# Sparse attention and a squared-ReLU MLP on one core: batch 3's strided heads on quarters of the array, wider sums and wider scaling

## The chip, the cores and the metric

The kernel runs on one core of one Trainium2 chip. The core has a matrix engine (TensorE, PE in the profile, with its weight loads as PEld), a vector engine (VectorE, DVE), a scalar engine for table functions (ScalarE, ACT), GpSimd (POOL), which here mostly issues transfers with a change of type, and SyncE (SP), which issues the other transfers and the transposes done by DMA. PSUM holds TensorE's results in eight banks of 512 fp32 columns by 128 partitions. The metric is the device time of one execution in microseconds; lower is better.

## The reference

Attention over 8 batches of 8 heads, 576 positions, head size 64, then an MLP over the 4608 resulting rows:

```python
rel = pos[:, None] - pos[None, :]
mask_local = (rel >= 0) & (rel < 32)
mask_strided = (rel >= 0) & (pos[None, :] % 32 == pos[:, None] % 32)
# heads 0..3 use mask_local, heads 4..7 mask_strided
attn = softmax(where(mask, 0.125 * q @ k.T, -1e9))
x = (attn @ v).transpose(0, 2, 1, 3).reshape(4608, 512)
r = maximum(x @ w_in, 0)          # w_in 512 x 2048
out = (r * r) @ w_out             # w_out 2048 x 512
```

A local head attends to the last 32 positions only. A strided head splits into 32 residue classes of 18 positions each; a position attends to the earlier ones of its own class. The kernel skips the rest.

## The kernel before

**Order of the work.** The MLP runs in nine chunks of 512 rows. A chunk has 16 groups of the first product (line 864: four matmuls of 512 columns into one bank, then a Relu on ScalarE, line 870, and a square on VectorE, line 874) and 16 of the second (line 970: four matmuls each; four groups make one output tile, copied by ScalarE, line 974, and stored over SP). These groups are numbered from 0 on, 32 to a chunk: groups 96 to 111 are the first product of chunk 3. The attention of batches 1 to 7 is cut into steps, and the text `PLAN`, written out by hand, says ahead of which group each step is issued. Batch b must be through before the chunk that holds its rows: batch 2 before group 64 (chunk 2), batch 3 before 96 (chunk 3), batch 4 before 128 (chunk 4). The chunk reads the strided rows of x, `xt[2]` and `xt[3]`, with the third and fourth matmul of a group. `tick()` runs after each group; `later(n, ...)` and `put_off(n, ...)` hold back a piece of a step by n groups, which the plan gives as numbers behind a plus sign.

**Banks.** Banks 4 and 5 alternate for the groups of both products. The other six are handed out in turn, singly (`bank`) or as neighbours (`bank_two`), to the attention steps.

**Strided heads, two ways.** The old way (batches 1 and 3, `OLD`) keeps K and V of two residue classes as block-diagonal 128 x 128 weights. `step_SS` (s3.0, s3.1, s3.2 in the plan) makes the scores of 8, 8 and 6 blocks of 54 columns with full-array matmuls (line 624) and takes Exp; `step_XX` (x3.0, x3.1, x3.2) makes the sums by one matmul with a block of ones (line 635), the values by one matmul a block (line 638), then 1/sum as Exp(-Ln(sum)) (lines 641, 643) and the products with it into `xt` (lines 651, 658). Two copies by VectorE fill the block-diagonal K (`step_K`, lines 380, 384) and two the V (`spread_v_str`, line 445).

The new way (batches 2, 4, 5, 6, 7) uses 64 x 64 quarters of the array, four matmuls at a time for four residue classes. `step_S4` makes 32 + 12 score matmuls (lines 688, 693) and three Exp; `step_X4` has three parts of 16, 16 and 12 value matmuls (line 757), each with four matmuls of ones for the sums (line 752) that share the bank of the values. `finish` then does, per part, Ln and Exp (lines 723, 724) and the products (line 736 for parts 0 and 1, six of 64 x 144 each; line 729 for part 2, four of 64 x 162). V comes by four DMAs into one of the two tiles of `vs_pool` (lines 430, 434); the old way takes two DMAs into a tile of its own (lines 438, 441).

**Local heads.** `step_G` makes the scores of four local heads with 24 matmuls into six banks (line 597), with six Exp (line 607) and the masks (line 604). `step_D` multiplies by V (line 823) and divides (lines 828, 829); `step_E` transposes into `xt` by DMA on SP from batch 2 on (line 838). `shift_v_local` (line 458) copies the 32 rows of V that overlap. In the plan, units 4b and 4b+1 are the two pairs of local heads of batch b: D16.0 is batch 4's first pair, first head.

The lines of the plan around the change (before):

```python
72: Q21k s3.0
...
75: x3.0
...
88: x3.1
90: x3.2
...
94: G4
...
99: X5k D16.0 D16.1
```

Of the kernel before, what the change touches and what calls it, by code (L numbers as in the profile page):

```python
# [8 lines left out]
FP32 = mybir.dt.float32  # L9
BF16 = mybir.dt.bfloat16  # L10
AF = mybir.ActivationFunctionType
# [51 lines left out]
50: Q17q Q16q s2  # L63
52: Q17k
55: X3k X3q
56: C4k C4q x2+2+4
57: V3 R12kv
58: V4 R12qa
60: B30v
61: B31v R13qv  # L70
62: R13ka
63: U4
64: X4q
66: Y17
67: Y16 C5q
68: k30v
69: k31v
70: X4k
71: C5k Q20k Q21q Q20q
72: Q21k s3.0  # L80
73: s3.1
75: x3.0
76: s3.2
80: G3
81: H3v
84: D12.0 D13.0
85: D12.1 D13.1
86: E12
87: E13
88: x3.1  # L90
90: x3.2
93: H4v
94: G4
96: k41v
97: Y20 Y21
98: U5
99: X5k D16.0 D16.1
100: C6k
101: X5q
102: Q25q V5  # L100
103: C6q
104: E16
106: s4 Q25k
107: D17.0
109: Q24k Q24q D17.1
111: E17
113: x4+2+5
114: k51v
122: G5
124: V6  # L110
127: H5v
# [5 lines left out]
138: D21.0  # L117
139: Q29k Q29q D21.1
142: E21
144: x5+2+5  # L120
150: H6v
152: k61v
154: G6
# [6 lines left out]
173: Y28  # L130
174: E24 D25.0 D25.1
175: Y29
176: x6+3+6
178: E25
187: H7v
188: G7
# [4 lines left out]
200: D28.1 E28  # L141
204: D29.1
206: E29
208: x7+4+8
"""

@with_exitstack
def kernel(
# [9 lines left out]
    nc = tc.nc  # L158
# [8 lines left out]
    NJ = 8  # L167
# [5 lines left out]
    NP2 = STRIDE // 2  # L173
    NG = 5
    NH = NG + 1
    OLD = (1, 3)
    NB = NP2 + NH
    NS = NP2 // 2
    W3 = 3 * NA
# [8 lines left out]
    att = ctx.enter_context(ExitStack())  # L188
    rows = ctx.enter_context(ExitStack())
    att_singles = att.enter_context(tc.tile_pool(name="att_singles", bufs=1))  # L190
    rv_pool = att.enter_context(tc.tile_pool(name="rv_pool", bufs=3))
    xl_pool = att.enter_context(tc.tile_pool(name="xl_pool", bufs=4))
    vs_pool = att.enter_context(tc.tile_pool(name="vs_pool", bufs=2))
    row_singles = rows.enter_context(tc.tile_pool(name="row_singles", bufs=1, side="right"))
# [27 lines left out]
    def bank_two():  # L222

        l = [id(t) for t in banks["pt"]]
        i = min((i for i in (0, 2, 6) if all(id(all_banks[i + j]) in l for j in range(2))),
                key=lambda i: max(l.index(id(all_banks[i + j])) for j in range(2)))
        for t in all_banks[i:i + 2]:
            k = [id(t) for t in banks["pt"]].index(id(t))
            banks["pt"].append(banks["pt"].pop(k))
            while id(t) in unread:  # L230
                run_due(lambda x: x[1] == unread[id(t)])
        return all_banks[i:i + 2], psb[:, i:i + 2]
# [27 lines left out]
    ones = singles.tile([128, D], BF16)  # L260
# [164 lines left out]
    def load_v_str(b):  # L425
        if b not in OLD:
            t = vs_pool.tile([128, (2 * NS + NH) * D], BF16, name="v_s")
# [186 lines left out]
    def blocks(part):  # L614
        return range(NJ * part, min(NJ * (part + 1), NB))
# [14 lines left out]
    def step_XX(b, part):  # L630
        run_due(lambda x: x[1] == (b, part))
        vb, n = vbd, len(blocks(part))
        e = es[2 + b % 2][:, NJ * W3 * part:NJ * W3 * part + W3 * n]
        pn, po = bank("pt")[:, 0:W3 * n], bank("pt")
        nc.tensor.matmul(pn, ones_bd, e, start=True, stop=True)
        for i, t in enumerate(blocks(part)):
            c = slice(W3 * i, W3 * (i + 1))
            nc.tensor.matmul(po[:, c], vb[:, t, :], e[:, c], start=True, stop=True)  # L638
        rv = rv_pool.tile([128, NJ * W3], FP32, name="rv")[:, 0:W3 * n]
        order = dict(a=n, h=3)  # L640
        nc.scalar.activation(rv.rearrange("c (h m a) -> c h m a", **order),
                             pn.rearrange("c (a h m) -> c h m a", **order), AF.Ln)
        nc.scalar.activation(rv, rv, AF.Exp, scale=-1.0)  # L643
        for h in (3,) if part == 2 else range(3):
            for par in range(2):
                r, x = slice(64 * par, 64 * par + 64), slice(64 * (h % 2), 64 * (h % 2) + 64)
                to = xt[2 + h // 2][x, b * S:(b + 1) * S].rearrange("c (m a r) -> c m a r", a=NP2, r=2)
                if part < 2:
                    of = po[r, 0:W3 * n].rearrange("c (a h m) -> c h m a", **order)[:, h]
                    by = rv[r].rearrange("c (h m a) -> c h m a", **order)[:, h]  # L650
                    nc.vector.tensor_tensor(to[:, :, NJ * part:NJ * (part + 1), par], of, by, op=ALU.mult)  # L651
                    continue
                of = po[r, 0:W3 * n].rearrange("c (a h m) -> c h m a", **order)
                by = rv[r].rearrange("c (h m a) -> c h m a", **order)
                for lo, g, k in ((0, 0, NG), (NG, 2, 1)):
                    t = to[:, :, 2 * NG * (g == 2) + lo, par]
                    t = bass.AP(t.tensor, t.offset, [t.ap[0], [2 * NG, 3 - g], [STRIDE, NA], [2, k]])
                    nc.vector.tensor_tensor(t, of[:, g:, :, lo:lo + k], by[:, g:, :, lo:lo + k], op=ALU.mult)
# [3 lines left out]
    def half(f, n=64):  # L662
        return slice(64 * f, 64 * f + n)
# [44 lines left out]
    def step_X4(b, pace):  # L708
        for part in range(3):
            run_due(lambda x: x[1] == ("s", b, part))  # L710
        for part in range(3):
            run_due(lambda x: x[1] == (b, part))
        e, vs = es[2 + b % 2], v_str[b]
        xb = slice(b * S, (b + 1) * S)

        def finish(part, n, both):
            w = n * W3
            rv = rv_pool.tile([128, NS * W3], FP32, name="rv")[:, 0:2 * w]
            pn = both[:, :, w:2 * w]
            o = "c (x f a) -> c f a x" if part < 2 else "c (f x a) -> c f a x"  # L720
            o, i = o.replace("f a x", "x f a") if part < 2 else o.replace("f a x", "f x a"), "c f (a x) -> c f a x"
            i = i.replace("c f a x", "c x f a" if part < 2 else "c f x a")
            nc.scalar.activation(rv.rearrange(o, f=2, a=n), pn.rearrange(i, a=n), AF.Ln)
            nc.scalar.activation(rv, rv, AF.Exp, scale=-1.0)  # L724
            if part == 2:
                for f, par in QUADS:
                    t = xt[3][64:128, xb]
                    t = bass.AP(t.tensor, t.offset + 2 * n * f + par, [t.ap[0], [2 * NG, 3], [STRIDE, NA], [2, n]])
                    nc.vector.tensor_tensor(t, both[half(par), f, 0:w].rearrange("c (a g m) -> c g m a", a=n, g=3),
                                            rv[half(par), w * f:w * (f + 1)].rearrange("c (g m a) -> c g m a", a=n, g=3),  # L730
                                            op=ALU.mult)
                return
            for h in range(3):
                for par in range(2):
                    to = xt[2 + h // 2][half(h % 2), xb].rearrange("c (m f a r) -> c m f a r", f=2, a=NS, r=2)
                    nc.vector.tensor_tensor(  # L736
                        to[:, :, :, n * part:n * (part + 1), par],
                        both[half(par), :, 0:w].rearrange("c f (a h m) -> c h m f a", a=n, h=3)[:, h],
                        rv[half(par)].rearrange("c (h m f a) -> c h m f a", h=3, f=2, a=n)[:, h], op=ALU.mult)

        due = []
        for part in range(3):
            n = (NS // 2, NS // 2, NH // 2)[part]
            w = n * W3
            pos, both = bank_two()

            def ecols(par, lo, k):
                c = NS * par + n * part + lo if part < 2 else 2 * NS + n * par + lo
                return slice(W3 * c, W3 * (c + k))

            for f, par in QUADS:
                nc.tensor.matmul(pos[f][half(par), w:2 * w], ones[half(f, W3)], e[half(f, W3), ecols(par, 0, n)],  # L752
                                 start=True, stop=True)
            for t in range(n):
                for f, par in QUADS:
                    r = 2 * (n * part + t if part < 2 else NS + t) + par
                    nc.tensor.matmul(pos[f][half(par), W3 * t:W3 * (t + 1)], vs[half(f, W3), D * r:D * (r + 1)],  # L757
                                     e[half(f, W3), ecols(par, t, 1)], start=True, stop=True)
            due.append((pace[part], pos, ("x", b, part), lambda part=part, n=n, both=both: finish(part, n, both)))
        for x in due:  # L760
            put_off(*x)

# [411 lines left out]
    for line in PLAN.strip().splitlines():  # L1174
        n, words = line.split(":")
# [42 lines left out]
```

## Time and profile before

| | us |
|---|---|
| median of 3 runs | 296.41 (296.08 to 297.07) |
| the profiled execution | 295.6 |
| its span, first to last instruction | 293.9 |
| TensorE busy (matmuls) | 286.8 |
| VectorE busy | 205.9 |
| ScalarE busy | 169.2 |
| GpSimd busy | 85.2 |

The profiled execution is one run; its span leaves out what lies before the first and after the last instruction. The granted clock of TensorE is full throughout (1.0). Matmuls overlap, so the mean duration of one is longer than the time from one to the next; the chain of work, which follows back from the last instruction what each piece waited for, gives the time that a piece adds. Names in the rows are those of the program: `psb` is PSUM, `xt` the MLP's input, `e` the exponentials, `rv` the reciprocals of the sums, `vb` and `kb` the block-diagonal weights.

### The profile page before, as it was taken

The page shows a single profiled execution, that of the slowest core. Times are in us where ns is not written, and L with a number is a line of the kernel's source. Part 1 is how long each engine was busy: PE and PEld are TensorE (multiplying, and loading weights), DVE is VectorE, ACT ScalarE, POOL GpSimd, SP SyncE. Part 2 cuts the span into 40 slices and gives each one's busy share as a digit, 9 for nine tenths or more (in the row PEclk, how much of TensorE's full clock was granted, in tenths as well). Part 3 has the DMA queues.
Part 4 walks back from the last instruction along what each step waited for, and adds up shares of the span by engine and source line. Part 5 has one row for each costly group of instructions (what it writes and reads, how often), then busy time and mean ns, then how long its engine had stood idle before and what let it go on. Part 6 is the DMA issues. An engine that isn't in the chain of part 4 may idle for free.

```text
span 293.9 us, 6454 instructions
## 1 busy us (share of the span) xinstructions
PE 286.8 (98%) x2477; PEld 153.0 (52%) x2477; DVE 205.9 (70%) x530; ACT 169.2 (58%) x318; POOL 85.2 (29%) x133
## 2 busy tenths in 40 slices
PE   6899999999999999999999999999999999999994
PEld 2554555544445454454445444444444444984594
DVE  5667798776587756667366826683389979958983
ACT  4767846684668736674577446654665566206610
POOL 8974442062116009246501740000000014103300
PEclk9999999999999999999999999999999999999999
DMA  7999999999999999999999999531011110030003
GB/s 151 180 209 207 197 203 180 159 243 127 153 220 130 172 163 185 164 129 125 217 204 109 158 183 165 86 58 74 36 20 55 75 38 0 1 117 30 0 2 143
DMA packets 91086, 37.23 MB, mean 127 GB/s; under 512 B 77392, under 2 KB 83896, under 8 KB 91056
## 3 DMA queue, kind: packets, MB, share of 16 engines
q0 software_dynamic: 49968, 18.14, 58.3%
q1 hardware_dynamic: 40944, 18.62, 34.0%
q8 instruction: 19, 0.31, 0.4%
q14 instruction: 11, 0.09, 0.1%
q10 hardware_dynamic: 144, 0.07, 0.1%
HBM read 36.83 MB, written 9.44 MB: 157 GB/s over the span
## 4 chain that ended last, share of the span: by engine, by line
PE 96%; DMA 2%; DVE 0%; issue 0%; DVEq 0%; POOLq 0%
PE psb L864 43%; PE psb L970 33%; PE psb L940 9%; DMA w_out_b<-in_q_dram 2%; PE psb L823 2%; PE psb L597 1%; PE psb L552 1%; PE psb L500 1%; PE psb L752 1%; PE psb L688 1%; PE psb L522 1%; PE psb L757 1%; PE psb L345 0%; PE psb L638 0%; PE psb L845 0%; PE psb L624 0%
## 5 line engine op out<-in xcount | busy, mean ns | idle before, releaser
L864 PE MATMUL psb<-xt,w_in 128*128 128x512 bf16 x576 | 131.9, 379 | 0.0
L870 ACT ACTIVATE r<-psb 128x512 bf16<-128x512 f32 x144 | 85.5, 598 | 46.0 <-PE psb L864 43.8
L970 PE MATMUL psb<-w_out_b,g_sb 128*128 128x512 bf16 x448 | 101.4, 379 | 0.0
L864 PEld LDWEIGHTS <-w_in 128*128 128x128 bf16 x576 | 53.8, 98 | 60.0 <-issue 0.8
L874 DVE TENSOR_TENSOR g_sb<-r 128x512 bf16<-128x512 bf16 x112 | 46.5, 422 | 39.9 <-ACT r L870 38.9
L970 PEld LDWEIGHTS <-g_sb 128*128 128x128 bf16 x448 | 41.8, 98 | 47.2
L974 ACT COPY y<-psb 128x512 f32<-128x512 f32 x28 | 16.6, 592 | 38.8 <-PE psb L970 38.7
L909 POOL CAST sa<-g_sb 128x256 fp32r<-128x256 bf16 x16 | 9.7, 605 | 96.5 <-DVE g_sb L904 96.5
L736 DVE TENSOR_TENSOR xt<-psb,rv 64x144 bf16<-64x144 f32 x60 | 18.7, 312 | 7.1 <-ACT rv L724 6.3
L604 DVE TENSOR_TENSOR e<-e,mask_all 128x576 bf16<-128x576 bf16 x24 | 10.0, 455 | 10.8 <-ACT e L607 10.7
L607 ACT ACTIVATE e<-psb 128x384 bf16<-128x384 f32 x36 | 15.0, 506 | 4.2 <-PE psb L597 4.2
L829 DVE TENSOR_TENSOR x_l<-psb,rinv 96x384 bf16<-96x384 f32 x28 | 15.5, 554 | 1.0
L904 DVE TENSOR_TENSOR g_sb<-r 128x512 bf16<-128x512 bf16 x32 | 13.0, 419 | 2.9 <-ACT r L870 2.9
L292 POOL DMA_DIRECT2D q_l<-in_q_dram x16 | 11.9, 749 | 9.3 <-PE psb L693 4.0
L363 POOL DMA_DIRECT2D q_t<-in_q_dram x6 | 3.2, 537 | 37.2 <-DMA qT_s<-q_t 35.5
L292 POOL DMA_DIRECT2D k_l<-in_k_dram x16 | 11.8, 741 | 1.5 <-issue 0.9
L940 PE MATMUL psb<-t,s 128*128 128x256 f32 x96 | 12.2, 283 | 0.0
L363 POOL DMA_DIRECT2D k_t<-in_k_dram x6 | 3.2, 538 | 30.1 <-DMA kT_s<-k_t 28.4
L940 PEld LDWEIGHTS psb<-t,s 128*128 128x128 f32 x96 | 11.6, 189 | 0.0
L952 DVE TENSOR_TENSOR y<-psb,y 128x256 f32<-128x256 f32 x19 | 8.1, 424 | 4.3 <-PE psb L940 3.5
L651 DVE TENSOR_TENSOR xt<-psb,rv 64x144 bf16<-64x144 f32 x24 | 7.5, 312 | 4.5 <-ACT rv L643 4.2
L823 PEld LDWEIGHTS <-e 128*128 128x128 bf16 x168 | 8.1, 97 | 4.8
(153 smaller groups left out, 316.8 us busy)
## 6 DMA issues: line engine op xcount, KB each, us to landing
out_dram<-y SPq DMA_DIRECT2D x35, 256.0 KB, 3.3
vl<-in_v_dram POOLq DMA_DIRECT2D x8, 288.0 KB, 8.5
w_out_b<-in_moe_w_out_dram POOLq DMA_DIRECT2D x4, 512.0 KB, 14.6
q_t<-in_q_dram POOLq DMA_DIRECT2D x7, 288.0 KB, 9.5
k_t<-in_k_dram POOLq DMA_DIRECT2D x7, 288.0 KB, 8.8
w_in<-in_moe_w_in_dram POOLq DMA_DIRECT2D x2, 768.0 KB, 13.5
k_l<-in_k_dram POOLq DMA_DIRECT2D x16, 72.0 KB, 6.9
q_l<-in_q_dram POOLq DMA_DIRECT2D x16, 72.0 KB, 7.7
```

The source lines that it names most:

```text
L292: nc.gpsimd.dma_start(out=t[:, :, hh, :], in_=src[b, 2 * p + hh].rearrange("(t p) d -> p t d", p=QL))
L607: nc.scalar.activation(e[:, row, 4 * QL * i:4 * QL * (i + 1)], bk[row][i][:, 0:4 * QL], AF.Exp, scale=scale)
L736: nc.vector.tensor_tensor(to[:, :, :, n * part:n * (part + 1), par], both[half(par), :, 0:w].rearrange("c f (a h m) -> c h m f a", a=n, h= ...
L823: nc.tensor.matmul(po[:, n, :], e[:, c:c + 128], rhs[:, NL * part + n, 0:D + 1], start=True, stop=True)
L829: nc.vector.tensor_tensor(x, po[0:QL, :, 0:D], rinv[0:QL].to_broadcast([QL, NL, D]), op=ALU.mult)
L864: nc.tensor.matmul(ph, w_in_tile(kk, ff), xt[kk][:, 512 * c:512 * (c + 1)], start=(kk == order[0]), stop=(kk == order[-1]))
L870: nc.scalar.activation(r, ph, AF.Relu)
L874: later(1, lambda: nc.vector.tensor_tensor(g[:, ff, :], r, r, op=ALU.mult))
L904: nc.vector.tensor_tensor(g[:, ff, :], r, r, op=ALU.mult)
L940: nc.tensor.matmul(pa, a, b, start=k == 0 and n not in "273", stop=k == 7, skip_group_check=True)
L970: nc.tensor.matmul(py, g[:, ff, 128 * j:128 * (j + 1)], w_out_b[:, ff, :], start=(ff == 0), stop=(ff == 15))
L974: nc.scalar.copy(y, py)
```

## The change

Batch 3 leaves the old way: its strided heads are done by `step_S4` and `step_X4`, and its steps in the plan become s3 at 72 and x3 at 88. The plan's steps for batch 4's local heads (G4, D16, D17, E16, E17) move, most of them later, and s4 and x4 by some groups. In `step_X4` parts 0 and 1 become one part of 32 value matmuls; its sums (four matmuls of 432 columns) go into a pair of banks of their own, and `finish` scales the whole part at once: one Ln and one Exp of 864 columns, and six products of 64 x 288. The last part, of 12 value matmuls, keeps its sums in the bank of its values. `rv_pool` has two larger tiles in place of three. The diff, cut to its core:

```diff
-56: C4k C4q x2+2+4
+56: C4k C4q x2+3
-60: B30v
-61: B31v R13qv
+61: R13qv
-68: k30v
-72: Q21k s3.0
-73: s3.1
-75: x3.0
-76: s3.2
+72: Q21k s3
-84: D12.0 D13.0
+83: D12.0 D13.0
-88: x3.1
-90: x3.2
+88: x3+1
-94: G4
-97: Y20 Y21
+97: Y20 Y21 G4+0+1+2+4+5+6
-99: X5k D16.0 D16.1
+99: X5k
-102: Q25q V5
+102: Q25q V5 D16.0
-104: E16
-106: s4 Q25k
-107: D17.0
-109: Q24k Q24q D17.1
-111: E17
-113: x4+2+5
-114: k51v
+104: D17.0
+106: Q25k D16.1
+107: D17.1 E16
+108: E17 s4
+109: Q24k Q24q
+114: k51v x4+3
-144: x5+2+5
+144: x5+3
-176: x6+3+6
+176: x6+4
-208: x7+4+8
+208: x7+5
...
-    OLD = (1, 3)
+    OLD = (1,)
...
-    rv_pool = att.enter_context(tc.tile_pool(name="rv_pool", bufs=3))
+    rv_pool = att.enter_context(tc.tile_pool(name="rv_pool", bufs=2))
...
-        def finish(part, n, both):
+        def finish(n, po, pn):
             w = n * W3
-            rv = rv_pool.tile([128, NS * W3], FP32, name="rv")[:, 0:2 * w]
-            pn = both[:, :, w:2 * w]
...
+            rv = rv_pool.tile([128, 2 * NS * W3], FP32, name="rv")[:, 0:2 * w]
+            o = "x f a" if n == NS else "f x a"
+            nc.scalar.activation(rv.rearrange(f"c ({o}) -> c {o}", f=2, a=n), pn.rearrange(f"c f (a x) -> c {o}", a=n), AF.Ln)
             nc.scalar.activation(rv, rv, AF.Exp, scale=-1.0)
...
-                        to[:, :, :, n * part:n * (part + 1), par],
-                        both[half(par), :, 0:w].rearrange("c f (a h m) -> c h m f a", a=n, h=3)[:, h],
+                        to[:, :, :, :, par],
+                        po[half(par)].rearrange("c f (a h m) -> c h m f a", a=n, h=3)[:, h],
                         rv[half(par)].rearrange("c (h m f a) -> c h m f a", h=3, f=2, a=n)[:, h], op=ALU.mult)
...
-        for part in range(3):
-            n = (NS // 2, NS // 2, NH // 2)[part]
+        for n, c0 in ((NS, 0), (NH // 2, 2 * NS)):
             w = n * W3
             pos, both = bank_two()
+            pns, bothn = bank_two() if n == NS else (pos, both)
+            po, pn = both[:, :, 0:w], bothn[:, :, 0:w] if n == NS else both[:, :, w:2 * w]
+            lo = 0 if n == NS else w
...
             for f, par in QUADS:
-                nc.tensor.matmul(pos[f][half(par), w:2 * w], ones[half(f, W3)], e[half(f, W3), ecols(par, 0, n)],
+                nc.tensor.matmul(pns[f][half(par), lo:lo + w], ones[half(f, W3)], e[half(f, W3), ecols(par, 0, n)],
                                  start=True, stop=True)
```

More of the change, by code (lines that the diff above doesn't have):

```diff
@@ L638, in step_XX @@
             nc.tensor.matmul(po[:, c], vb[:, t, :], e[:, c], start=True, stop=True)
-        rv = rv_pool.tile([128, NJ * W3], FP32, name="rv")[:, 0:W3 * n]
+        rv = rv_pool.tile([128, 2 * NS * W3], FP32, name="rv")[:, 0:W3 * n]
         order = dict(a=n, h=3)
@@ L714, in step_X4 @@
         xb = slice(b * S, (b + 1) * S)
-        def finish(part, n, both):
+        def finish(n, po, pn):
             w = n * W3
-            rv = rv_pool.tile([128, NS * W3], FP32, name="rv")[:, 0:2 * w]
-            pn = both[:, :, w:2 * w]
[L720 to L723, printed above, removed]
+            rv = rv_pool.tile([128, 2 * NS * W3], FP32, name="rv")[:, 0:2 * w]
+            o = "x f a" if n == NS else "f x a"
+            nc.scalar.activation(rv.rearrange(f"c ({o}) -> c {o}", f=2, a=n), pn.rearrange(f"c f (a x) -> c {o}", a=n), AF.Ln)
             nc.scalar.activation(rv, rv, AF.Exp, scale=-1.0)
-            if part == 2:
+            if n < NS:
                 for f, par in QUADS:
@@ L728, in finish @@
                     t = bass.AP(t.tensor, t.offset + 2 * n * f + par, [t.ap[0], [2 * NG, 3], [STRIDE, NA], [2, n]])
-                    nc.vector.tensor_tensor(t, both[half(par), f, 0:w].rearrange("c (a g m) -> c g m a", a=n, g=3),
+                    nc.vector.tensor_tensor(t, po[half(par), f].rearrange("c (a g m) -> c g m a", a=n, g=3),
                                             rv[half(par), w * f:w * (f + 1)].rearrange("c (g m a) -> c g m a", a=n, g=3),
@@ L736, in finish, with ecols @@
                     nc.vector.tensor_tensor(
-                        to[:, :, :, n * part:n * (part + 1), par],
-                        both[half(par), :, 0:w].rearrange("c f (a h m) -> c h m f a", a=n, h=3)[:, h],
+                        to[:, :, :, :, par],
+                        po[half(par)].rearrange("c f (a h m) -> c h m f a", a=n, h=3)[:, h],
                         rv[half(par)].rearrange("c (h m f a) -> c h m f a", h=3, f=2, a=n)[:, h], op=ALU.mult)
         due = []
-        for part in range(3):
-            n = (NS // 2, NS // 2, NH // 2)[part]
+        for n, c0 in ((NS, 0), (NH // 2, 2 * NS)):
             w = n * W3
             pos, both = bank_two()
-            def ecols(par, lo, k):
-                c = NS * par + n * part + lo if part < 2 else 2 * NS + n * par + lo
+            pns, bothn = bank_two() if n == NS else (pos, both)
+            po, pn = both[:, :, 0:w], bothn[:, :, 0:w] if n == NS else both[:, :, w:2 * w]
+            lo = 0 if n == NS else w
+            def ecols(par, t, k):
+                c = c0 + n * par + t
                 return slice(W3 * c, W3 * (c + k))
             for f, par in QUADS:
-                nc.tensor.matmul(pos[f][half(par), w:2 * w], ones[half(f, W3)], e[half(f, W3), ecols(par, 0, n)],
+                nc.tensor.matmul(pns[f][half(par), lo:lo + w], ones[half(f, W3)], e[half(f, W3), ecols(par, 0, n)],
                                  start=True, stop=True)
@@ L755, in step_X4 @@
                 for f, par in QUADS:
-                    r = 2 * (n * part + t if part < 2 else NS + t) + par
+                    r = c0 + 2 * t + par
                     nc.tensor.matmul(pos[f][half(par), W3 * t:W3 * (t + 1)], vs[half(f, W3), D * r:D * (r + 1)],
                                      e[half(f, W3), ecols(par, t, 1)], start=True, stop=True)
-            due.append((pace[part], pos, ("x", b, part), lambda part=part, n=n, both=both: finish(part, n, both)))
+            due.append((pace[len(due)], pos if n < NS else pos + pns, ("x", b, n),
+                        lambda n=n, po=po, pn=pn: finish(n, po, pn)))
         for x in due:
```

## The prediction

> **What bounds the kernel now.** I read the page first: its busy line, then the chain that ended last. Then I read that chain in order of time, because TensorE is nearly the whole of it and the size of each gap is what counts. The groups by line and form came third, for durations, and the timeline last, around the places where the chain runs long. 0.3% of this kernel, 0.89 us, is about what a measurement can tell from no change.
>
> ```profile
> span 293.9 us, 6454 instructions
> PE 286.8 (98%) x2477; PEld 153.0 (52%) x2477; DVE 205.9 (70%) x530; ACT 169.2 (58%) x318; POOL 85.2 (29%) x133
> PE 96%; DMA 2%; DVE 0%; issue 0%; DVEq 0%; POOLq 0%
> ```
>
> TensorE is busy 98% of the span and 96% of the chain. An edit therefore gains only what it takes off TensorE's own queue, and loses only where TensorE comes to wait. The chain, in order of time (start, duration, what), shows both:
>
> ```profile
> 57.56 0.77 PE psb L597 x24
> 58.34 4.42 PE psb L864 x20
> ...
> 67.82 1.73 PE psb L970 x8
> 69.54 0.37 PE psb L688 x32
> 69.91 0.10 PE psb L693 x12
> 70.01 5.29 PE psb L970 x24
> 75.30 0.22 PE psb L752 x4
> 75.51 0.12 PE psb L757 x16
> 75.63 0.10 PE psb L752 x4
> 75.73 0.12 PE psb L757 x16
> 76.02 7.01 PE psb L970 x32
> 83.03 7.02 PE psb L864 x32
> 90.05 0.20 PE psb L624 x8
> ...
> 91.11 0.20 PE psb L624 x8
> ...
> 93.04 0.18 PE psb L635
> 93.23 0.21 PE psb L638 x8
> ...
> 94.30 0.15 PE psb L624 x6
> 94.46 3.52 PE psb L864 x16
> ...
> 106.34 0.18 PE psb L635
> 106.52 0.21 PE psb L638 x8
> ...
> 108.47 0.14 PE psb L635
> 108.60 0.16 PE psb L638 x6
> ...
> 112.22 0.62 PE psb L597 x24
> ...
> 114.66 2.68 PE psb L864 x12
> ```
>
> Undisturbed, a matmul of the projections takes 1.73 / 8 = 0.216 us. By that rate 32 of them take 6.92, 24 take 5.19, 20 take 4.32, 16 take 3.46 and 12 take 2.59. So the pieces that follow work on quarters or halves of the array (70.01, 76.02, 58.34) run 0.10 over: that is what a change of array shape costs. Three other excesses have another cause, since no change of shape stands there: 0.10 at 83.03, 0.06 at 94.46 and 0.09 at 114.66.
>
> **The change, part by part.**
>
> *Batch 3 on TensorE.* Removed are its score blocks (0.20 + 0.20 + 0.15 = 0.55) and its sums and values (0.39 + 0.39 + 0.30 = 1.08; the last rows of each part end 0.01 later in the full chain and I leave that), 1.63 us in all, with no charge for a change of shape. Added is what batch 2 shows for the same steps: scores 0.37 + 0.10, with 0.10 for the shape, 0.57; sums and values from 75.30 to 76.02, 0.72, with 0.09 after them, 0.81. Together 1.38. Gain 0.25.
>
> *Sums in banks of their own, six batches.* Parts 0 and 1 become one part. The sums' two groups, 4 matmuls of 216 columns each, become one of 4 matmuls of 432; the 44 value matmuls stay. Before, the two groups cost 0.22 + 0.10. The wide group is not in the trace. If fixed cost ruled, it would take 0.22 and each of six batches would gain 0.10 (0.60 in all). If the columns rule, it takes 0.22 + 0.10 and gains nothing. The full-array sums take 0.18 for 432 columns (106.34) and 0.14 for 324 (108.47), in proportion to columns, so I take 0.32, no gain, and keep 0.22 for the low end. The banks are three pairs as before. The second pair is wanted some 0.2 us earlier. I cost that at nothing, since the blocks ahead of these steps were read long before; where local blocks stand just ahead (batch 6) the pair written last is still needed at the same time.
>
> *Scaling 288 columns at a time.* Per batch, ScalarE's two Ln and two Exp of 432 columns become one of each of 864, and twelve VectorE products of 144 become six of 288. The groups by form (busy us, mean ns):
>
> ```profile
> L724 ACT ACTIVATE rv<-rv 128x432 f32<-128x432 f32 x10 | 5.6, 562 | 0.3
> L723 ACT ACTIVATE rv<-psb 128x432 f32<-128x432 f32 x10 | 5.2, 523 | 0.6 <-PE psb L757 0.6
> L723 ACT ACTIVATE rv<-psb 128x324 f32<-128x324 f32 x5 | 2.2, 446 | 0.0
> L736 DVE TENSOR_TENSOR xt<-psb,rv 64x144 bf16<-64x144 f32 x60 | 18.7, 312 | 7.1 <-ACT rv L724 6.3
> L829 DVE TENSOR_TENSOR x_l<-psb,rinv 96x384 bf16<-96x384 f32 x28 | 15.5, 554 | 1.0
> L729 DVE TENSOR_TENSOR xt<-psb,rv 64x162 bf16<-64x162 f32 x20 | 9.4, 468 | 1.0 <-ACT rv L724 0.4
> L658 DVE TENSOR_TENSOR xt<-psb,rv 64x270 bf16<-64x270 f32 x4 | 2.5, 621 | 0.7 <-ACT rv L643 0.6
> ```
>
> Ln grows by (523 - 446) / 108 = 0.71 ns a column, so 432 more cost 0.31: Ln 0.83 and Exp 0.87. The first product starts 0.62 later than now. A product of 288 lies between 0.312 (one of 144, no dearer) and 288 x 621 / 270 = 0.66. Between the rows of 144 and of 384, a straight line gives 0.457. I take that, because L736, the same operation on half the columns, is one of its two ends. With 0.013 between products, as now, six take 2.82 against twelve in 3.90: 1.08 less.
>
> Off the path this costs nothing, except where a batch is late for its chunk. Batch 2 is. The timeline of its products, and of two other waits:
>
> ```profile
> 76.98 1.95 DVE L736 TENSOR_TENSOR xt<-psb,rv 64x144 bf16<-64x144 f32 x6 [3.81 <-ACT rv L724]
> ...
> 82.61 0.97 DVE L729 TENSOR_TENSOR xt<-psb,rv 64x162 bf16<-64x162 f32 x2
> ...
> 85.65 0.55 POOL L363 DMA_DIRECT2D k_t<-in_k_dram  x1 [10.92 <-DMA kT_s<-k_t]
> ...
> 112.52 2.40 ACT L607 ACTIVATE e<-psb 128x384 bf16<-128x384 f32 x6 [1.41 <-PE psb L597]
> ```
>
> VectorE runs without a gap from 76.98 to 83.58 there, and chunk 2's first output wants the strided rows with its third and fourth matmul, 0.43 to 0.65 after its start: the 0.10 at 83.03 is this wait. The new end is 83.58 + 0.62 - 1.08 = 83.12, and the last part is put off 3 groups instead of 5, so its reciprocals are there in time. The stall of 0.10 goes. It would stay if a product took over 0.53 ((83.58 - 0.10 - 83.12) / 6 above 0.47).
>
> *Batch 3 as one late step.* Its three score steps become one at group 72; its three value steps (75, 88, 90) become one at 88. The Ln and Exp that stood in chunk 2's up-projection at 75 leave it, and with them the 0.06 at 94.46. In return all of its scaling comes after 88. Counting as for batch 2: 1.68 from the first sum to the first product, plus 0.62, then 2.82, then four products of 0.49: 7.08 us. Chunk 3 wants it after 0.81 + 8 x 0.865 + 0.65 = 8.38. That hides it, with 1.3 us to spare, unless a product takes over 0.69. What would be late next is the shift of batch 4's local V rows on VectorE, three groups ahead of chunk 3, and its first use is past group 102.
>
> *Batch 4's local steps moved.* Scores go from 94 to 97, behind the start of chunk 3, their six Exp spread over 0, 1, 2, 4, 5, 6 groups; the value blocks go from 99, 99, 107, 109 to 102, 106, 104, 107; the transposes to 107 and 108, the strided scores to 108, the strided values to 114. TensorE's own cost moves unchanged (0.62 + 0.10). Now the six Exp take ScalarE from 112.52 for 2.40, right before chunk 3's first Relu: that is the 0.09 at 114.66, and it goes. Batch 2 shows the spread form at 57.56, with the same spacing: 20 matmuls behind it run 4.42, no more than the 0.10 for the shape. Its own 0.77 instead of 0.62 I take for its key copy, which batch 4 has not got; 0.15 lost is the bound. The two output transposes pass nothing on SP's queue: the four transposes of batch 5's local rows and the two of its strided rows stay ahead of them, and chunk 4 wants them 20 groups later. The POOL loads keep their order. The six banks of these scores include batch 3's last pair, read 7.08 us after batch 3's first sum and wanted no sooner than 0.81 + 9 x 0.865 = 8.6 after it. Batch 3's own first value blocks come one group earlier (83 for 84), after a mask that is due at 82: nothing.
>
> *Loads and copies.* Batch 3's V now comes by four DMAs instead of two, into the two-buffer pool that the other batches share. On POOL two more issues cost, by the rows of these same loads,
>
> ```profile
> L434 POOL DMA_DIRECT2D v_s<-in_v_dram x10 | 6.3, 630 | 3.1 <-DMA xt<-in_q_dram 1.4 <-DMA xt<-in_k_dram 0.9 <-DMA k_l<-in_k_dram 0.8
> L430 POOL DMA_DIRECT2D v_s<-in_v_dram x10 | 5.4, 540 | 2.7 <-DMA w_out_b<-in_moe_w_out_dram 2.2 <-issue 0.5
> ```
>
> 1.17 us. Queued behind them are four loads of batch 4's local rows, whose transposes come past group 66, and then POOL sits idle 10.92 us (85.65) for a transpose: hidden; without that cover it would be 1.17 late for batch 4's keys. Batch 4's V waits for batch 2's values, batch 5's for batch 3's, both issued groups earlier. The copies that spread batch 3's K and V (VectorE) go; no piece of the chain waits for them, so nothing is gained. The reciprocals' tiles are two instead of three: batch 1's third part then waits for the products of its first, which stand two parts ahead of it on VectorE: nothing.
>
> **The sum.** 0.25 + 0 + 0.10 + 0.06 + 0.09 = 0.50 us. The profiled execution took 295.6 with its span of 293.9, and would take 295.1; the median of the three runs is 0.81 above it, so the forecast is 296.41 - 0.50 = 295.9.
>
> **The rivals.**
>
> More is gained: the wide sums cost 0.22 (0.60 over six batches), with the 0.50: 295.3. For it: the first group's 0.22 is half fixed cost. Against it: the proportion in the full-array rows.
>
> The stalls only move: the three go and come back behind other steps, and batch 4's scores keep batch 2's 0.15: 296.41 - 0.25 + 0.15 = 296.3.
>
> Slower: ScalarE becomes the bound in chunk 3. Relu leaves it little per group of 0.865, and an Exp takes 2.40 / 6 = 0.40. If the spread Exp hold up the Relus, TensorE waits for a bank: the price is from nothing to the whole 2.40, without the 0.09: 296.41 - 0.41 + 2.40 = 298.4, at two thirds of it 297.6. It decides when more than 1.3 us shows. Against it: batch 2's row at 58.34. For it: in chunk 3 batch 4's strided scores follow with three more Exp, which batch 2's chunk (chunk 1) had not.
>
> Slower too: quarter-array matmuls start no faster than full ones. A full block of 54 columns takes 0.20 / 8 = 0.025. At that rate 88 take 2.2, the wide sums 4 x 0.18, the narrow 4 x 0.07, with the shape 0.2, 3.4 against 1.63: 296.41 + 1.77 - 0.25 = 297.9. The row against it: 44 in 0.47, 0.011 each.
> The Trainium skill (TensorE: Matmul & The Clock Gate, "Wait — 56ns, not 53.3ns?") says that start to start never drops below about 25 ns, however few the columns; by that rule 88 matmuls would take 2.2 us, this rival's time. By that rule, the trace disagrees: 0.011 us each on quarters.
>
> Products of 288 at 0.66 instead of 0.46: batch 2 ends 6 x 0.21 = 1.24 later, at 84.36, where chunk 2 can wait until 83.47: a stall of 0.89, so 296.41 - 0.40 + 0.89 = 296.9.
>
> **How the numbers follow.** Forecast as summed 0.42 (its own range 295.5 to 296.3); more gained, past 0.3%, 0.25; stalls move 0.08 and slow products 0.06, both within 0.3%; ScalarE as bound past 0.3% 0.16; quarter matmuls one by one 0.03. That makes faster 0.25, same 0.56, slower 0.19. The range goes from 295.1, the second case with a little of the runs' spread, to 297.3, which leaves out the upper cases.
>
> **What would show it.** Batch 3's scores as 32 + 12 matmuls in 0.47 us; the first sums of each batch near 0.32; products of 288 near 0.46 us; no excess in the first chunk-2 piece; batch 3's last product over 1 us ahead of chunk 3; Relus in chunk 3 on time. Wrong it would be if matmul groups of chunk 3 run over 0.865 us beside the Exp, or if products take over 0.53.

## The result and the profile after

The changed kernel takes 295.1 us (median, 294.75 to 295.72) beside 296.69 for the kernel before (296.08 to 298.87): ratio 0.9949, 95% interval 0.9924 to 0.9974, so faster by 1.6 us in the medians. The two profiled executions lie much closer: 295.08 against 295.6, spans 293.4 and 293.9. A third of the gain, then, can be read from this pair of profiles; the rest lies between the profiled execution of before and its median. That gap, which the prediction carried along as 0.81 us, has closed: the changed kernel's profiled execution is at its median. Ratios and counts of runs here and below leave out single runs over 1.5% above the fastest of their kernel (granted clock 0.972 to 0.994); the medians and ranges in tables hold them.

From the page of the changed kernel:

```profile
span 293.4 us, 6453 instructions
PE 287.2 (98%) x2506; PEld 152.5 (52%) x2506; DVE 199.9 (68%) x489; ACT 167.0 (57%) x306; POOL 86.7 (30%) x135
```

The chain of the changed kernel in order of time (start, duration, what). Line 743 is the sums, 748 the values (the chain lists 11 of the last 12), 680 and 685 the strided scores, 589 the local scores, 856 and 962 the two products of a chunk:

```profile
51.52 0.86 PE psb L856 x4
...
75.46 0.31 PE psb L743 x4
75.77 0.25 PE psb L748 x32
76.02 0.10 PE psb L743 x4
76.12 0.09 PE psb L748 x11
76.21 7.01 PE psb L962 x32
83.22 6.91 PE psb L856 x32
90.12 0.37 PE psb L680 x32
90.50 0.10 PE psb L685 x12
90.59 7.04 PE psb L856 x32
...
105.99 0.31 PE psb L743 x4
106.30 0.25 PE psb L748 x32
106.55 0.10 PE psb L743 x4
106.65 0.09 PE psb L748 x11
106.74 7.01 PE psb L962 x32
113.75 0.86 PE psb L856 x4
114.62 0.62 PE psb L589 x24
115.23 4.42 PE psb L856 x20
...
289.83 0.42 DVE y L940
```

Against the undisturbed 6.92 for 32 matmuls: chunk 2's first piece (83.22) is clean, where it ran 7.02 before. Batch 3's scores are 0.47 with 0.12 behind them, its sums and values 0.75 with 0.09. Behind batch 4's local scores 20 matmuls take 4.42, only the 0.10 of a change of shape, so the spread Exp hold up nothing. From the start of chunk 1 (51.35 before, 51.52 after) to the last product (289.97, 289.83) the chain is 238.62 before and 238.31 after: 0.31 us. The start was 0.17 slower in this execution.

The groups by line and form of the changed kernel (busy us, mean ns):

```profile
L725 DVE TENSOR_TENSOR xt<-psb,rv 64x288 bf16<-64x288 f32 x36 | 17.3, 479 | 14.3 <-ACT rv L713 13.9
L713 ACT ACTIVATE rv<-rv 128x864 f32<-128x864 f32 x6 | 5.5, 923 | 0.2
L712 ACT ACTIVATE rv<-psb 128x864 f32<-128x864 f32 x6 | 5.3, 890 | 1.5 <-PE psb L743 1.5
```

A product of 288 columns takes 0.479 us, one Ln and one Exp of 864 columns 1.81 together.

Before's chain, the start of chunk 1 and the last row:

```profile
51.35 0.86 PE psb L864 x4
...
289.97 0.42 DVE y L948
```

From the end of this product to the end of the span, 3.5 us pass before (293.9 - 290.39) and 3.15 after (293.4 - 290.25). No step of the change stands there. These 0.35 us and the runs above the profiled one are what the experiments had to explain.

### The profile page after: what moved, and what is told of

It reads as the page before. It is cut to its first block, busy times and chain, and to the rows that moved or that the text cites. A ratio compares the mean times of both kernels' runs of the same rounds, so it can differ in the third digit from the quotient of the medians.

```text
span 293.4 us, 6453 instructions
## 1 busy us (share of the span) xinstructions
PE 287.2 (98%) x2506; PEld 152.5 (52%) x2506; DVE 199.9 (68%) x489; ACT 167.0 (57%) x306; POOL 86.7 (30%) x135
## 4 chain that ended last, share of the span: by engine, by line
PE 96%; DMA 2%; DVE 0%; issue 0%; DVEq 0%; POOLq 0%
PE psb L856 43%; PE psb L962 33%; PE psb L932 9%; DMA w_out_b<-in_q_dram 2%; PE psb L815 2%; PE psb L589 1%; PE psb L544 1%; PE psb L492 1%; PE psb L743 1%; PE psb L680 1%; PE psb L748 1%; PE psb L514 1%; PE psb L337 0%; PE psb L837 0%; PE psb L327 0%
## 5 line engine op out<-in xcount | busy, mean ns | idle before, releaser
L725 DVE TENSOR_TENSOR xt<-psb,rv 64x288 bf16<-64x288 f32 x36 | 17.3, 479 | 14.3 <-ACT rv L713 13.9
L718 DVE TENSOR_TENSOR xt<-psb,rv 64x162 bf16<-64x162 f32 x24 | 11.2, 469 | 1.2 <-ACT rv L713 0.5
L443 POOL DMA_DIRECT2D vl<-in_v_dram x8 | 9.8, 1226 | 3.8 <-DVE xt L718 2.9
```

Source lines behind the costliest of these rows:

```text
L718: nc.vector.tensor_tensor(t, po[half(par), f].rearrange("c (a g m) -> c g m a", a=n, g=3), rv[half(par), w * f:w * (f + 1)].rearrange("c ( ...
L725: nc.vector.tensor_tensor(to[:, :, :, :, par], po[half(par)].rearrange("c f (a h m) -> c h m f a", a=n, h=3)[:, h], rv[half(par)].rearrang ...
```

## The experiments

All ran in five rounds beside the kernel before on the same chip; kernels that went together share its runs.

| kernel | median (lowest to highest) | before, same chip | ratio (95%) |
|---|---|---|---|
| before again | 295.91 (295.40 to 300.57) | 296.0 | 1.0004 (0.9978 to 1.0030) |
| wide sums and scaling alone | 296.23 (295.12 to 300.28) | 296.0 | 1.0001 (0.9979 to 1.0023) |
| changed, narrow again | 296.72 (296.02 to 302.11) | 296.0 | 1.0019 (0.9999 to 1.0038) |
| batch 4's steps moved alone | 296.79 (295.82 to 300.36) | 296.0 | 1.0007 (0.9985 to 1.0029) |
| changed again | 295.06 (294.73 to 296.71) | 296.56 | 0.9960 (0.9940 to 0.9981) |
| batch 3's V in four transfers alone | 295.39 (295.02 to 295.85) | 296.56 | 0.9968 (0.9952 to 0.9984) |
| the same, second time | 295.73 (294.98 to 296.43) | 296.45 | 0.9969 (0.9948 to 0.9991) |
| its small part in three pieces | 295.83 (295.26 to 296.49) | 296.45 | 0.9974 (0.9956 to 0.9993) |
| batch 3's V load earlier | 296.41 (295.45 to 302.73) | 296.45 | 0.9979 (0.9947 to 1.0011) |
| batch 7's V in three pieces | 295.82 (295.34 to 299.97) | 296.46 | 0.9978 (0.9956 to 0.9999) |
| before, batch 2's output on TensorE | 297.73 (297.20 to 298.28) | 296.56 | 1.0047 (1.0027 to 1.0067) |
| changed, the same edit | 296.85 (296.55 to 297.51) | 296.56 | 1.0017 (1.0000 to 1.0033) |

### Is the gain there again?

Kernel before, no edit:

> The kernel before, unchanged, run as a kernel of its own. Its purpose is the gap between the two profiles (chain of work 0.3 us shorter) and the two sets of times (medians 1.6 us apart). Theory Q (the gain is TensorE's queue, 0.3 us, and the rest is the spread of the runs): ratio 1.000 within 0.003, a profile like the first one with no excess over 0.1 us outside changes of array shape except the three known ones (chunk 2's first piece 0.10, 0.06 and 0.09 later), and the changed kernel would come out 0.3 to 0.5 us faster than this one when run beside it. Theory W (the kernel before waits in many executions where its one profile did not): its profile shows TensorE waiting somewhere for 0.5 us or more that the first profile did not have, and its runs spread over 1 us or more.

The changed kernel, no edit:

> The changed kernel again, beside runs of the kernel before on the same chip. Theory Q (TensorE's queue alone, 0.3 us on the chain): ratio 0.9985 to 0.9995, and the first comparison's 0.9949 was partly the spread of the runs of before. Theory W (in many executions of before TensorE waits at chunk 2's start for the transposes of batch 2's local output, as in the profiles of the wide-only kernel, 0.58 us, and of the moved-only kernel, 1.02 us): ratio 0.996 or less, the lowest runs of both kernels only 0.3 to 0.5 us apart, the medians over 1 us apart, and no excess over 0.1 us at chunk 2's first group in this profile.

The gain is there again: 0.9960. Before against itself gives 1.0004, with a profile that repeats the first one's excesses and has none of the waits that theory W wanted, so the gap isn't an accident of one comparison. The chains repeat too: from the start of chunk 1 to the last product, 238.60 in before again and 238.29 in the changed kernel again, 0.31 us as at first. The lowest runs are 0.73 us apart (295.46 and 294.73), the medians 1.5. The 0.73 is more than either theory had, and about what the chain's 0.31 and the 0.35 to 0.4 at the end make together; the other 0.8 comes from executions of before that run longer.

### The three parts that the prediction had priced

The wide step alone, in the kernel before:

```diff
-56: C4k C4q x2+2+4
+56: C4k C4q x2+3
...
-        for part in range(3):
-            n = (NS // 2, NS // 2, NH // 2)[part]
+        for n, c0 in ((NS, 0), (NH // 2, 2 * NS)):
```

> The kernel before with the wide sums and the wide scaling alone (batches 2, 4, 5, 6, 7); batch 3 stays on block-diagonal weights and batch 4's local steps stay where they were. Theory Q: each wide step costs TensorE 0.03 us more than the two narrow ones (0.31 against 0.22 + 0.10 for the sums, 0.75 against 0.72 in all), 0.15 over five batches; chunk 2's first piece loses its 0.10 excess; together 0.05 slower to 0.05 faster, ratio 1.000. Theory W with the products' lateness as the wait: 1.0 us faster or more, ratio 0.997 or less, since batch 2's products end 0.4 us earlier.

Ratio 1.0001: as theory Q had it, no gain of its own. But its profile caught a wait that the first two had not. The row of waits on TensorE in this kernel, and its chain there:

```profile
PE psb L864 <- DMA xt<-x_l: 0.4, 1, 0.4
```

```profile
74.88 8.76 DMA xt<-x_l
...
83.69 6.85 PE psb L864 x31
```

Chunk 2 waits for a transpose of batch 2's local output (`step_E`). In before's first profile the two had landed at 79.2 and 81.2 (68.9 + 10.3 and 72.2 + 9.0), the second 1.8 us ahead of chunk 2. Here the second was issued at 74.88, 2.7 later; its 8.76 us to land are no more than before's. So this wait comes from the late issue: SP took 6.5 us from 70.3 to issue the two, for 5.5 from 68.9 in before.

The changed kernel with narrow sums and scaling put back, and the kernel before with batch 4's steps moved:

```diff
-88: x3+1
+88: x3+1+2
...
-        for n, c0 in ((NS, 0), (NH // 2, 2 * NS)):
+        for part in range(3):
+            n = (NS // 2, NS // 2, NH // 2)[part]
```

> The changed kernel with the narrow sums and narrow scaling put back in all six batches: batch 3 on quarters and batch 4's local steps moved, nothing else. Theory Q: batch 3 gains 0.20 to 0.25, the 0.06 and the 0.09 go, chunk 2's first piece keeps its 0.10: 0.35 to 0.40 us faster than before, ratio 0.9987. Theory W with the products' lateness as the wait: no more than that, while the changed kernel is 1.5 us faster; theory W with the moved or removed steps as the wait: 1.2 us faster or more, ratio 0.996.

```diff
-94: G4
-97: Y20 Y21
+97: Y20 Y21 G4+0+1+2+4+5+6
...
-106: s4 Q25k
+106: Q25k D16.1
+107: D17.1 E16
+108: E17 s4
-113: x4+2+5
-114: k51v
+114: k51v x4+2+5
```

> The kernel before with batch 4's steps moved as in the change (scores at 97 spread over six groups, value blocks, transposes, strided steps), nothing else. Theory Q: the 0.09 excess at chunk 3's start goes, ratio 0.9997. Theory W with batch 4's early scores as the wait: 1 us faster or more. The rival of the prediction, ScalarE as the bound in chunk 3: slower by 0.8 to 2.4 us, with groups of chunk 3 over 0.865 us beside the spread Exp.

Neither gains; both came out slower than theory Q had it. The 0.9997 of the moved steps lies within their interval, the 0.9987 of the narrow version outside its own (0.9999 to 1.0038). The chain of the narrow version shows where its 0.3 to 0.4 went:

```profile
83.03 7.02 PE psb L856 x32
90.05 0.37 PE psb L680 x32
...
138.99 0.49 PE psb L589 x17
139.48 0.33 PE psb L589 x7
...
290.15 0.42 DVE y L940
```

Chunk 2's 0.10 is back, as expected of narrow scaling. Batch 5's local scores take 0.82 instead of the 0.62 that they take in the changed kernel. I put that down to banks: narrow scaling, put off 2 and 5 groups from 114 on, may still be reading what these scores want at 122 (no row names the wait). That 0.2 us the wide step saves, and I had not priced it. The rest is no part of the steps that I had priced: in the last chunk VectorE stood 0.7 us without a releaser, for which the chain is some 0.3 longer, and from the last product to the end it is 3.8 us (294.4 - 290.57). VectorE's row:

```profile
DVE y L944 <- issue: 0.7, 1, 0.7
```

The trace's DMA records hold 8 KB of instructions that load from 281.33 to 281.74, and VectorE goes on at 281.75. That suggests that it waited for them, but one case does not show it. With these 0.5 us on the chain and 0.7 at the end, the narrow version is 0.6% behind the changed kernel (1.0019 and 0.9960), though the wide step alone had been worth nothing.

The moved steps' profile, of an execution of 298.0 us, caught the same wait for batch 2's output, larger, and a second one inside batch 2's values that nothing in the profile releases:

```profile
PE psb L862 <- DMA xt<-x_l: 0.9, 1, 0.9
PE psb L755 <- issue: 0.6, 1, 0.6
```

The rival that ScalarE becomes the bound fails here too: behind the spread Exp 20 matmuls take 4.42 in this kernel as well.

### The load of batch 3's V

The one part of the change left was the load of batch 3's V, two transfers before and four after. Alone, in the kernel before:

```diff
-        nc.gpsimd.dma_start(out=t[:, 0:RW], in_=v[b, 4:7]...)
...
+        k = 2 if b == 3 else 1
+        w, wh = RW // k, 2 * (NG + 1) * D // k
+        for f in range(k):
+            nc.gpsimd.dma_start(out=t[:, w * f:w * (f + 1)], in_=v[b, 4:7]...[:, w * f:w * (f + 1)])
+            ...
+            nc.gpsimd.dma_start(out=t[:, RW + wh * f:RW + wh * (f + 1)], in_=src)
```

> The kernel before with one edit: batch 3's V is loaded by four transfers with rows half as long instead of two, into the same tile. Theory L (the split load is why the transposes of batch 2's output land earlier in the changed kernel, 6.6 us after issue instead of 9.0 to 10.3): those transposes land in under 7.5 us, and the median falls by 0.5 us or more against before, ratio under 0.9985. Theory Q and theory W without L: ratio 1.000 within 0.002, landing times of 8 to 14 us as in the other kernels.

> The kernel before with batch 3's V by four transfers, again, beside the other two on one chip. Theories W and T together: ratio 0.996 to 0.998, median within 0.4 us of its lowest run, 3.85 us from the last matmul to the end. If the first result was the luck of a chip: ratio over 0.999.

0.9968 and 0.9969: this edit, which I had priced at nothing, brings about 0.9 us by the ratios (the medians are 1.17 and 0.72 apart), with the chain of TensorE's work as before in the first of its profiles (238.63). Its page and the last row of its chain:

```profile
span 293.5 us, 6457 instructions
```

```profile
289.95 0.42 DVE y L952
```

3.13 us from the last product to the end, 0.4 less than before. And its highest run is 295.85 (296.43 the second time), where before, by the runs counted, reaches 297.92 and 299.52. The second time the median lies 0.75 above the lowest run, though, not within the 0.4 expected. The transposes of batch 2's output took 6.9 and 8.0 us to land in the first of these kernels and 8.3 and 8.7 in the second; theory L's 7.5 doesn't hold, while the gain is much the same. Three more edits asked what in it does this: the row length, the place, or the number of transfers.

Only the small transfer split, in three, so as many transfers, with the long rows whole:

```diff
...
-        nc.gpsimd.dma_start(out=t[:, RW:2 * NB * D], in_=src)
+        n = 3 if b == 3 else 1
+        w = 2 * (NG + 1) * D // n
+        for f in range(n):
+            s7 = bass.AP(src.tensor, src.offset + w * f, [[2 * NG * D, 3], [RW, NA], [1, w]])
+            nc.gpsimd.dma_start(out=t[:, RW + w * f:RW + w * (f + 1)], in_=s7)
```

> The kernel before with the small one of batch 3's two V loads (81 KB) in three pieces and the large one whole: as many transfers and instructions as with both loads split in two, but the long rows stay. Theory T: the time from the last matmul to the end falls from 4.23 to 3.85 us and the median by about 0.4, ratio 0.9985, with the spread of before. Theory W with the row length as the cause: the spread of before and the transposes of batch 2's output landing after 8.5 us or more; with both theories true, exactly these two together. If it comes out like the split load (0.9968, median within 0.4 of the lowest), the row length is not the cause and the number or order of transfers is.

0.9974, highest run 296.49, transposes after 7.5 and 9.1 us, and the shorter end:

```profile
span 294.0 us, 6421 instructions
```

```profile
290.43 0.42 DVE y L951
```

(294.0 - 290.85 = 3.15; 36 matmul records are missing from this trace's count.) The long rows of the large transfer are not the cause.

The two transfers as they were, issued earlier:

```diff
-33: T8kv
+33: T8kv U3
...
-47: U3 D8.1
+47: D8.1
```

> The kernel before with the load of batch 3's V issued at group 33 instead of 47, ahead of the loads that wait for batch 2's strided transposes; its form (two transfers with long rows) and the number of instructions stay. Theory W (the load's traffic holds back the transposes of batch 2's output, for which chunk 2 then waits in many executions): these transposes land in under 8 us, the median comes within 0.4 us of the lowest run (before: 0.8 to 1.1), the lowest stays within 0.2 of before's, ratio 0.997 to 0.999; from the last matmul to the end of the span it stays 4.2 us. Theory T (the split load's gain is only the tail, 0.4 us, since two more instructions shift where instructions are fetched): no change, ratio 1.000 and the same spread.

No gain that can be told (0.9979, interval up to 1.0011), the spread of before (3 of 10 runs over 297, before 7 of 28), and 3.5 us at the end. Its profiled execution, at 298.0, shows what one long execution holds. Landing times of batch 2's two transposes, the waits of TensorE, and further on in its chain:

```profile
DMA to landing us min/median/max: 12.3/12.3/12.4
```

```profile
PE psb L864 <- DMA xt<-x_l: 0.6, 1, 0.6
PE psb L624 <- DVE g_sb L874: 0.8, 1, 0.8
```

```profile
113.87 3.28 DMA xt<-x_l
117.19 2.53 PE psb L864 x11
```

Chunk 2 waits for batch 2's transposes, batch 3's scores (line 624) then longer still for VectorE's copies of its key, whose transposes took 11.48 us to land, and chunk 3 for batch 3's output. So late transfers of more than one kind stand in this execution, and moving the load earlier does not remove them.

Two more transfers, but far away, in batch 7's local V:

```diff
-        nc.gpsimd.dma_start(out=t[32:128, ...], in_=v[b, 0:4]...)
+        to, src = t[32:128, ...]..., v[b, 0:4]...
+        n = 3 if b == 7 else 1
+        w = 4 * NL // n
+        for f in range(n):
+            nc.gpsimd.dma_start(out=to[:, w * f:w * (f + 1)], in_=src[:, w * f:w * (f + 1)])
```

> The kernel before with the load of batch 7's local V (group 156, long after chunk 2) in three pieces instead of one: two more transfers, as in the kernels with batch 3's V split, but far from batch 2's output and chunk 2. Theory N (the number of instructions alone gives both the shorter end and the narrower spread): 0.4 us less from the last product to the end of the span, ratio 0.996 to 0.998, highest run under 297. Theory P (pieces matter where chunk 2's transfers are in flight; the number alone gives the shorter end): the end 0.4 us shorter, the lowest run 0.3 to 0.4 lower than before's, but a quarter of the runs over 297 as before, ratio 0.998 to 0.9995.

The end is shorter here too:

```profile
span 293.8 us, 6457 instructions
```

```profile
290.28 0.42 DVE y L951
```

(293.8 - 290.70 = 3.10.) So two more transfers take the 0.4 us off the end wherever they stand: in the four such profiles with TensorE's program as it was, it is 3.1 to 3.15, in the six profiles with the old number (before twice, the wide step, the moved steps, the earlier load, and before with the edit of the next section) 3.4 to 3.6.

The packed traces show where these 0.4 us stand: in GpSimd's last instructions, which no view lists. Once the stores have landed, GpSimd is released, runs an instruction named DRAIN, clears the semaphores, and the program ends. In five of the six profiles with the old number the DRAIN starts 0.37 to 0.39 us after the release and takes 0.24 to 0.25; in all eight profiles with two more transfers it starts after 0.08 and takes 0.10 or 0.11. That is 0.44 us. (The sixth, the wide step alone, has 0.08 and 0.17, but its release comes some 0.25 later after the last product.) In the same six an 8 KB load of instructions starts at the end of the span, within 0.04 us; in the eight others the last one starts 11.9 us or more before it. That load comes after the DRAIN and can't have held it up; what did is not shown.

The other half is not settled. One of 11 runs lies over 297, at 297.38, against none of 36 in the three runs with batch 3's V in more pieces, and 5 of 17 for before. The ratio, 0.9978, lies at the edge of theory N's range, and its interval covers the other kernels'. And the narrow version speaks against both theories: it loads batch 3's V in four transfers and has GpSimd's short DRAIN, yet 4 of its 11 runs lie over 297 and its ratio is 1.0019. Its long end is another one: GpSimd is released 3.19 us after the last product there, 2.40 to 2.68 elsewhere, since the last stores land later.

### Taking the wait away

Batch 2's local output transposed by TensorE, in the kernel before and in the changed one:

```diff
-        if b >= 2:
+        if copy is None:
             nc.sync.dma_start_transpose(
...
-48: Q16k D9.1 E8
-49: E9
+48: Q16k D9.1 E8a
+49: E9a
```

> The kernel before with batch 2's local output transposed by TensorE (two times six 96 x 96 transposes, 0.26 us each, and a ScalarE copy) instead of by transfers, so chunk 2 can't wait for these transfers. Theory Q: 0.5 us slower in every run, ratio 1.0018, the spread of the runs unchanged. Theory W: lowest run 0.5 us slower, but the spread shrinks (median less than 0.5 us above the lowest, where before has 0.8), so the median is the same or lower, ratio 0.998 to 1.000.

> The changed kernel with the same edit of batch 2's local output. Theory Q: 0.5 us slower than the changed kernel. Theory W: the changed kernel doesn't wait there, so this one is 0.5 us slower than it, and about 0.3 us faster than the kernel before with the same edit: with the wait taken out of both, only TensorE's queue tells them apart.

The cost was mis-sized: not 0.5 but 1.2 us in before's median and 1.8 in the changed kernel's; TensorE now stands 1.1 us for the division just ahead of the transposes. Of theory W's signs the narrower spread came (297.20 to 298.28), the ratio up to 1.000 did not. With chunk 2's wait out of both, the changed kernel is still 0.88 faster (297.73 and 296.85), where I expected 0.3. The chains, from the start of chunk 1 to the last product, in before and in the changed kernel with this edit:

```profile
51.09 0.86 PE psb L864 x4
...
291.45 0.42 DVE y L948
```

```profile
51.93 0.86 PE psb L856 x4
...
291.87 0.42 DVE y L940
```

That is 240.36 and 239.94, 0.42 less, and the end takes 3.6 and 3.2 us (295.5 - 291.87 and 295.5 - 292.29), 0.4 less: together the 0.8 that the medians show. The two profiled executions took the same time (297.20 and 297.21) because the start of the second was 0.84 us slower.

## Why the prediction was right and where it was not

The time, 295.1, lies at the very end of the range, and the sign is as forecast; the size, 1.6 us beside a forecast of 0.5 (0.8 against the median of the forecast, 295.9), is not. That the range holds it is luck: its low end was set by the rival of sums at 0.22, and the sums took 0.31.

*TensorE's queue.* Batch 3 on quarters: forecast 0.25; 0.47 + 0.12 + 0.75 + 0.09 = 1.43 against 1.63, so 0.20. The shape's charge of 0.10 stands.

*Wide sums.* The choice of 0.32 for the wide group was right: 0.31. The rest of the step grew a little, 0.75 against 0.72 in all, 0.03 in four batches and 0.01 in batch 6 (0.79 against 0.78): a loss of 0.13 where I had nothing.

*Products.* 0.479 against 0.457 and under the 0.53 at which it would have failed. Ln and Exp took 1.81 instead of 1.70. The 0.10 at chunk 2 went, and it came back when the narrow sums and scaling did, which bears out the lateness of the products as its cause. It went by little: batch 2's last product ends at 83.52 and is wanted at 83.65 (83.22 and two matmuls). Batch 3's ends at 113.35, only 0.40 ahead of chunk 3 and 0.83 ahead of the matmul that wants it, where I had set over 1 us. The 0.06 went (7.04 holds the shape's 0.10), and so did the 0.09.

*The rival that ScalarE becomes the bound* fell: 4.42 behind the spread scores, and 0.62 for them, not 0.77. So did matmuls one by one: 44 in 0.47 again.

These terms add to 0.20 - 0.13 + 0.10 + 0.06 + 0.09 = 0.32, and the chain shows 0.31. On the profiled execution the forecast was 295.1 and 295.08 came, but partly by another term than mine: 0.31 on the chain less 0.17 at the start, and 0.35 at the end.

*The step that failed* is "Loads and copies": two more issues on POOL, "hidden". Their own 1.17 us was hidden indeed. What I had not asked is what else two more transfers change: GpSimd's last instructions take 0.44 us less, and alone, in the kernel before, the two bring 0.9 us. With the chain's 0.31 that makes 0.9968 x (1 - 0.31 / 296) = 0.9958, and the changed kernel beside them came to 0.9960. The sizes fit, but the two parts need not add: the narrow version has the same four transfers and gains nothing.

*The offset* was the second fault of the same kind. I carried the 0.81 us between profile and median over as if it belonged to the runs. It did not stay when the kernel changed. My reading is that in longer executions chunk 2 waits for transposes that the profiled one received in time. Three profiles of variants show that wait, of 0.4 to 0.9 us, and the two longest of them, both 298.0, other waits of 0.6 and 0.8 beside it; of the changed kernel neither profile does. But neither of the two profiles of before shows it, so for the kernel before itself this is argued, not shown.

So of the 1.5 to 1.6 us, 0.31 on the chain and 0.4 at the end are shown. The other 0.8, the long executions of before, stays open: batch 3's V in more pieces keeps them away in the kernel before, neither the large transfer's long rows nor the late issue of the load is the reason, and the narrow version has them in spite of its four transfers. Where instructions are loaded differs between these programs and was not tested. What holds up GpSimd's DRAIN in the kernels with the old number stays open too.

## What to carry to other kernels

A single profile says what one execution waited for. When the median lies well above it, the gap is a term of its own, and transfers that land not far ahead of their use (here 1.8 us) are a place to look for it. An edit priced at nothing because its own time is hidden should still be run alone: here, alone, it brought more than all that had a price (0.9 and 0.31 us). And an edit's gain should be tried in the changed kernel too, not only in the kernel before: the parts did not add here. To tell half a percent, sum the chain in both kernels from the same step on, with start and end apart.

## What the runs showed of the hardware

The time from the last product to the end of the span went with the program: 3.4 to 3.6 us in six profiles of before and the variants with its number of transfers, 3.1 to 3.2 in seven of kernels with two more, 3.8 in the narrow version, each with the same last stores. GpSimd's DRAIN and the gap ahead of it take 0.62 to 0.63 us of it in five of the first six and 0.18 to 0.19 in the eight others. Four matmuls of ones on quarters take 0.31 us for 432 columns where 216 took 0.22 or 0.10. A transpose by transfer of the same 96 rows, issued at nearly the same time, landed after 6.6 us in one kernel and 12.3 in another.
